# Reordering the first loads, adding filler matmuls and fixing two GpSimd steps in a fused retention and adapter kernel

## The chip, the core and the metric

The kernel runs on one core of a Trainium2 chip. The core has five engines with a queue each. TensorE (PE in the profile, with its weight loads as PEld) multiplies matrices. VectorE (DVE) and ScalarE (ACT) move and combine tiles. GpSimd (POOL) does slower elementwise work and issues its own DMAs. SyncE (SP) does nothing here but issue DMAs. The metric is the device time of one execution in microseconds (us); lower is better.

## The reference: what is computed

Two parts follow each other. The first is causal retention for 8 batches, 8 heads, 576 positions and head size 64, all fp32:

```python
scores = scale * np.matmul(q, k.transpose(0, 1, 3, 2))
Dmat = np.where(rel >= 0, gamma[:, None, None] ** rel[None, :, :], 0.0)   # rel = i - j
attn = np.matmul(scores * Dmat, v)
x = attn.transpose(0, 2, 1, 3).reshape(4608, 512)
```

The second is a mixture of eight low-rank adapters. Each row x gets gate logits `x @ w_gate`. The two largest are kept and weighted by a softmax over the two, and the row receives `x + sum of w_e * (x @ A[e]) @ B[e]`, where A[e] is 512 x 16 and B[e] is 16 x 512.

## The kernel before, in words

The 576 positions are cut into four chunks of 128 and one of 64. A chunk of four batches is a "quad", which is loaded together, and two batches of a quad are a "unit". `units` lists 16 full units and, for the last chunk, two of half length. Every unit goes through lettered stages. T transposes q and k on PE with the identity `id64`. S multiplies kT by qT into `ps`, and DVE applies the causal mask (`rt`). U accumulates the state `pu` from k and v. Q multiplies the carried state P by qT. R multiplies rt by v into `px`, and DVE scales that into `xT`. Z multiplies `xT` by the packed adapter matrices and gate weights `AW` (`pz`), V and W route, B and X transpose, and Y multiplies by `Bcat` (the B matrices as fp16) and stores the rows.

PE, DVE and ACT instructions are emitted through `mm`, `vec` and `act` (lines 80 to 87). Each of them calls `chain` (line 73), which ties an instruction to the one before it on the same engine, so the order on these three engines is that of the source. GpSimd instructions are emitted directly, with `gp.`, and are not chained: there the framework's scheduler picks the order within what the data allow. SP's DMAs go out in the order in which the program places them.

The steps that matter here all lie in the first 45 us:

- `issue(0)` (line 195) loads the first quad in pieces: q and k of batch 0, of batch 1, then v of both, then the adapter matrix A (`load_A`, line 170), then q, k and v of batches 2 and 3. Its local `load` takes the issuing engine as an argument; k of batches 0 and 1 goes through ACT's queue (line 230), all else through SP's. `issue(1)` and later calls load a whole quad, 1 MB for each of q, k, v, from SP.
- At line 651 `spin(10)` sends ten fp16 matmuls of a zero tile (`idle`) into an unused bank (`spare`), ahead of the first real work.
- `first_T` (line 295) transposes the first unit batch by batch: q of batch 0, k of batch 0, q of batch 1, k of batch 1, eight transposes each. ACT copies qT out of the accumulators and DVE copies kT.
- `scale_k` (line 253) makes GpSimd scale k in place, one instruction for a batch, after PE has transposed it. `stage_U` needs the scaled k.
- `fill_pick` (line 620) builds the selector `pick` on GpSimd in four steps. `place_A` (line 173) uses it on PE to lay A out, and ACT copies the result into `AW[0]`. The gate weights are loaded straight into `AW[0]` by a GpSimd DMA (line 655). GpSimd then copies `AW[0]` with its halves swapped into `AW[1]` (lines 669 and 670), and line 671 loads `Bcat` with a GpSimd DMA that converts to fp16.
- After the first four units, lines 699 to 703 make two small masks `maskh` on GpSimd, which nothing uses before the last two units.

Of the kernel before, what the change touches and what calls it, by code (L numbers as in the profile page):

```python
# [18 lines left out]
def kernel(  # L19
# [10 lines left out]
    nc = tc.nc  # L30
# [26 lines left out]
    for hp in range(HP):  # L57
        for ho in range(2):
            g = gam[2 * hp + ho]
            r = slice(64 * ho, 64 * ho + 64)  # L60
# [12 lines left out]
    def chain(eng, i):  # L73

        i = getattr(i, "ins", i)
        if eng in queued:
            tc.add_manual_dep(i, queued[eng].name, order, reason="program order")
        queued[eng] = i

    def mm(*args, **kw):  # L80
        chain("pe", nc.tensor.matmul(*args, **kw))  # L81
# [20 lines left out]
    def bank(shape, name, dtype=FP32):  # L102

        n = free.pop(0)
        x = pp.tile(shape, dtype, tag=f"bank{n}", name=name)
        held[id(x)] = n, x
        return x

    def done(*tiles):
        free.extend(held.pop(id(x))[0] for x in tiles)  # L110
# [5 lines left out]
    gp = nc.gpsimd  # L116
# [3 lines left out]
    for base in (0, -L):  # L120
        gp.affine_select(
            out=id64, in_=id64, compare_op=ALU.not_equal, fill=1.0, base=base,
# [4 lines left out]
        out=tri, in_=tri, compare_op=ALU.is_ge, fill=0.0, base=0,  # L127
# [6 lines left out]
        out=ident16, in_=ident16, compare_op=ALU.not_equal, fill=1.0, base=0,  # L134
        pattern=[[-1, 128]], channel_multiplier=1,
    )
    for g in range(2):
        gp.tensor_copy(
            out=trih[64 * g : 64 * g + 64], in_=tri[64 * g : 64 * g + 64, 64 * g : 64 * g + 64]
# [7 lines left out]
    def spin(n):  # L147

        for _ in range(n):
            mm(spare, lhsT=idle[:, 0:128], rhs=idle, start=True, stop=True)  # L150
# [11 lines left out]
    AW = [  # L162
        cpool.tile([128, HP, ER + E], FP32, tag=f"AW{g}", name=f"AW{g}") for g in range(2)
    ]
    Bcat = cpool.tile([128, Dm], FP16, tag="Bcat", name="Bcat")
# [4 lines left out]
    def load_A():  # L170
        nc.sync.dma_start(out=Arow, in_=moe_A.rearrange("e (p l) r -> p e (l r)", l=4))
# [23 lines left out]
    def issue(n):  # L195
        if n >= len(quads):
            return
        c, qd = quads[n]
        first = n == 0
        tl = [  # L200
            iop.tile([128, QUAD, H, Dh], FP32, tag=tag, name=tag, bufs=n)
            for tag, n in (("q32", 2), ("k32", 3), ("v32", 3))
        ]
        if c == NFULL:
            if qd > 0:
                return
            for src, dst in zip((q, k, v), tl):
                for g in range(2):
                    nc.sync.dma_start(
                        out=dst[64 * g : 64 * g + 64].rearrange("p s h d -> p (s h) d"),  # L210
                        in_=src[HALF * g : HALF * g + HALF, :, C * c : C * c + L, :].rearrange(
                            "s h j d -> j (s h) d"
                        ),
                    )
            for u in range(2):
                nat[(c, u, 0)] = [x[:, 2 * u : 2 * u + 2] for x in tl]
            return

        def load(n, lo, hi, eng=nc.sync):
            eng.dma_start(  # L220
                out=tl[n][:, lo:hi].rearrange("p b h d -> p (b h) d"),
                in_=(q, k, v)[n][
                    QUAD * qd + lo : QUAD * qd + hi, :, C * c : C * c + C, :
                ].rearrange("b h j d -> j (b h) d"),
            )

        if first:
            for b in range(2):
                load(0, b, b + 1)
                load(1, b, b + 1, nc.scalar)  # L230
            load(2, 0, 2)
            load_A()
            for n in range(3):
                load(n, 2, 4)
        else:
            for n in range(3):
                load(n, 0, 4)
        for sl in range(2):
            nat[(c, qd, sl)] = [x[:, 2 * sl : 2 * sl + 2] for x in tl]
# [7 lines left out]
    def rows(g):  # L247
        return slice(64 * g, 64 * g + 64)
# [46 lines left out]
    def first_T():  # L295

        s = st.setdefault(0, {})
        for nm in ("qT", "kT"):
            s[nm] = wk.tile([128, 2, HP, C], FP32, tag=nm, name=nm, bufs=4 if nm == "qT" else 2)
        for b in range(2):  # L300
            for n, nm in enumerate(("qT", "kT")):
                src = nat[units[0]][n]
                ps = [bank([128, HP, L], f"p{nm}") for _ in range(2)]
                for hp in range(HP):
                    for g in range(2):
                        mm(
                            ps[g][:, hp, :],
                            lhsT=src[rows(g), b, 2 * hp : 2 * hp + 2, :],
                            rhs=id64[rows(g), :],
                            is_transpose=True,  # L310
                            start=True,
                            stop=True,
                        )
                for g in range(2):
                    o = s[nm][:, b, :, rows(g)]
                    if n == 0:
                        act("copy", out=o, in_=ps[g])
                    else:
                        vec("tensor_copy", out=o, in_=ps[g])
                done(*ps)  # L320

    def stage_Q(t):
        c, qd, sl = units[t]
# [296 lines left out]
    def fill_pick(*dts):  # L620
# [9 lines left out]
        out=asc[0].rearrange("p a (m n) -> p a m n", n=NI),  # L630
# [16 lines left out]
    for t in range(NU):  # L647
        if units[t][2] == 0:
            issue(quads.index(units[t][:2]) + 2)
        if t == 0:  # L650
            spin(10)
            first_T()
            scale_k(0)
            fill_pick(3)
            gp.dma_start(
                out=AW[0][:, :, ER : ER + E], in_=moe_w_gate.rearrange("(t p) e -> p t e", p=128)
            )
            for ho in range(2):
                act("copy", out=asc[1][rows(ho)], in_=asc[0][rows(1 - ho)])
            act(  # L660
                "copy", out=gdec.rearrange("p a b d -> p a (b d)"),
                in_=gde.unsqueeze(2).broadcast_to((128, HP, 2 * Dh)),
            )
            stage_S(0)
            stage_U(0)
            stage_Q(0)
            stage_R(0)
            place_A()
            for ho in range(2):
                gp.tensor_copy(out=AW[1][rows(ho)], in_=AW[0][rows(1 - ho)])  # L670
            gp.dma_start(out=Bcat, in_=moe_B.rearrange("e r d -> (e r) d"))
            stage_T(1, ("qT",))
            stage_T(1, ("kT",), shared=True)
            scale_k(1)
            stage_Z(0)
            stage_S(1)
            stage_W(0)
            stage_U(1)
            stage_Q(1)
            stage_R(1)  # L680
            stage_T(2, ("qT",))
            stage_B(0)
            stage_X([0])
            stage_Z(1)
            stage_V(1)
            stage_Y(0, spread=True)
            stage_T(2, ("kT",), shared=True)
            stage_T(3)
            scale_k(2)
            scale_k(3)  # L690
            stage_S(2)
            stage_W(1)
            stage_S(3)
            for u in (2, 3):
                stage_U(u)
                stage_Q(u)
                stage_R(u)
            late_T(4)
            for ho in range(2):
                gp.tensor_tensor(  # L700
                    out=maskh[ho], in0=trih.unsqueeze(1).broadcast_to((128, HP, L)),
                    in1=heads(1, ho, L), op=ALU.mult,
                )
            continue
        if t < 4 or units[t][2] or not is_full(t):
            continue

        before, near = [u for u in (t - 4, t - 3) if u > 0], (t - 2, t - 1)
        here = (t, t + 1)
        for u in here:  # L710
            for b, nm in enumerate(("qT", "kT")):
                stage_S(u, (b,))
                if t > LATE:
                    stage_T(u + 2, (nm,))
            if t > LATE:
                scale_k(u + 2)
        for u in before:
            stage_B(u)
        stage_X(before)
        stage_Z(near[0])  # L720
        stage_V(near[0])
        for u in before:
            stage_Y(u)
        stage_Z(near[1])
        stage_V(near[1])
        if units[t][0] > 0:
            for u in here:
                stage_Q(u)
        for u in near:
            stage_W(u)  # L730
        for u in here:
            stage_U(u)
            if units[t][0] == 0:
                stage_Q(u)
            stage_R(u)
        if t <= LATE:
            late_T(t + 2)

    h, n = NU - 2, NU - 1
# [66 lines left out]
```

## Time and profile before

| What | us |
|---|---|
| Median of five runs (lowest 184.71, highest 187.22) | 185.24 |
| The profiled execution, whole | 187.22 |
| Its span, from the first to the last instruction | 185.5 |
| PE busy in the span | 175.3 |
| DVE busy | 115.5 |
| ACT busy | 66.7 |
| POOL busy | 58.1 |

In the profile, a row of the timeline gives the start, the length, the engine, the line, the operation, and the tiles as "written <- read"; "x8" means eight instructions merged, and the bracket tells how long the engine had been idle before and what ended the wait. Line 81 is `mm`, line 84 `vec` and line 87 `act`, so PE, DVE and ACT rows are told apart by tile names. Matmuls overlap, so a group's length includes the tail of its last one; the distance between the starts of two groups is what PE spends on the first. The profiled execution is the slowest of the five, 1.98 us above the median, and about 1.7 us of its time lie outside the span.

### The profile page before, as it was taken

The page shows a single profiled execution, that of the slowest core. Times are in us where ns is not written, and L with a number is a line of the kernel's source. Part 1 is how long each engine was busy: PE and PEld are TensorE (multiplying, and loading weights), DVE is VectorE, ACT ScalarE, POOL GpSimd, SP SyncE. Part 2 cuts the span into 40 slices and gives each one's busy share as a digit, 9 for nine tenths or more (in the row PEclk, how much of TensorE's full clock was granted, in tenths as well). Part 3 has the DMA queues.
Part 4 walks back from the last instruction along what each step waited for, and adds up shares of the span by engine and source line. Part 5 has one row for each costly group of instructions (what it writes and reads, how often), then busy time and mean ns, then how long its engine had stood idle before and what let it go on. Part 6 is the DMA issues. An engine that isn't in the chain of part 4 may idle for free. (4 is left out here: it accounts for less than half of the span.)

```text
span 185.5 us, 8103 instructions
## 1 busy us (share of the span) xinstructions
PE 175.3 (94%) x3606; PEld 163.8 (88%) x3606; DVE 115.5 (62%) x294; ACT 66.7 (36%) x179; POOL 58.1 (31%) x69
## 2 busy tenths in 40 slices
PE   7997999969999999999999999999999999999970
PEld 2796999959999999999999999999999999999850
DVE  3684956967578745866267816792578347485660
ACT  3512146024412334087511753075406460132440
POOL 8685108026016600588022621453050004000000
PEclk9999999999999999999999999999999999999995
DMA  6999898869698989797899899998940050033185
GB/s 145 278 248 248 238 299 236 223 168 291 183 302 237 286 258 282 201 287 259 245 283 348 256 255 323 253 202 178 255 151 4 0 222 11 4 111 124 58 256 144
DMA packets 53283, 38.74 MB, mean 209 GB/s; under 512 B 26992, under 2 KB 48640, under 8 KB 53248
## 3 DMA queue, kind: packets, MB, share of 16 engines
q1 hardware_dynamic: 50688, 37.23, 71.0%
q10 hardware_dynamic: 2384, 0.85, 1.8%
q8 instruction: 28, 0.46, 1.1%
q0 software_dynamic: 176, 0.15, 0.5%
q14 instruction: 7, 0.06, 0.1%
HBM read 28.91 MB, written 9.44 MB: 207 GB/s over the span
## 5 line engine op out<-in xcount | busy, mean ns | idle before, releaser
L84 DVE TENSOR_TENSOR rt<-ps,mask 128x512 f32<-128x512 f32 x64 | 40.3, 684 | 9.2 <-PE ps L81 8.0
L259 POOL TENSOR_TENSOR k<-k,pack 128x512 f32<-128x512 f32 x32 | 32.6, 1043 | 28.2 <-PE pkT L81 21.3
L81 PE MATMUL pz<-AW,xT 128*128 128x136 f32 x288 | 37.2, 282 | 0.0
L418 POOL TENSOR_TENSOR P<-pn,gdec 128x512 f32<-128x512 f32 x12 | 15.3, 1278 | 68.5 <-DVE pn L84 64.3
L81 PEld LDWEIGHTS pz<-AW,xT 128*128 128x128 f32 x288 | 34.7, 190 | 0.2
L81 PE MATMUL ps<-qT,kT 64*128 64x128 f32 x512 | 34.7, 278 | 0.1
L81 PEld LDWEIGHTS ps<-qT,kT 64*128 64x128 f32 x512 | 31.4, 188 | 1.2 <-issue 0.5
L81 PE MATMUL px<-rt,v 128*64 128x128 f32 x512 | 30.7, 273 | 0.0
L87 ACT COPY qT<-pqT 128x512 f32<-128x512 f32 (+1 forms) x33 | 16.8, 568 | 31.4 <-PE pqT L81 31.4
L81 PEld LDWEIGHTS px<-rt,v 128*64 128x64 f32 x512 | 27.7, 137 | 0.0
L84 DVE TENSOR_TENSOR xT<-px,asc 128x512 f32<-128x512 f32 x36 | 24.4, 689 | 3.9 <-PE px L81 2.6
L87 ACT COPY kT<-pkT 128x512 f32<-128x512 f32 x29 | 16.0, 600 | 29.4 <-PE pkT L81 18.7
L84 DVE COPY lg<-pz 128x16 f32<-128x16 f32 x17 | 3.0, 174 | 32.9 <-PE pz L81 32.9
L81 PE MATMUL pu<-v,k 128*64 128x64 f32 x512 | 18.1, 224 | 0.0
L87 ACT COPY osb<-po 128x256 f32<-128x256 f32 x60 | 17.5, 386 | 1.4 <-PE po L81 0.8
L81 PEld LDWEIGHTS pu<-v,k 128*64 128x64 f32 x512 | 16.6, 138 | 1.4 <-issue 1.0
L87 ACT ACTIVATE sg<-lg,ns 128x8 f32<-128x8 f32 x34 | 8.4, 293 | 25.3 <-DVE ns L84 24.9
L81 PE MATMUL pkT<-id,k 64*128 64x64 f32 x288 | 13.3, 227 | 3.1 <-DMA k<-in_k_dram 3.0
L81 PEld LDWEIGHTS pkT<-id,k 64*128 64x128 f32 x288 | 11.7, 141 | 4.3 <-issue 2.2
L81 PE MATMUL px<-qT,P 64*64 64x128 f32 (+1 forms) x512 | 14.2, 259 | 0.0
L84 DVE TENSOR_TENSOR pn<-pu,P 128x512 f32<-128x512 f32 x12 | 8.3, 692 | 8.3 <-PE pu L81 8.3
L81 PEld LDWEIGHTS px<-qT,P 64*64 64x64 f32 x512 | 12.5, 133 | 0.9
(54 smaller groups left out, 151.6 us busy)
## 6 DMA issues: line engine op xcount, KB each, us to landing
out_dram<-osb SPq DMA_DIRECT2D x32, 256.0 KB, 4.2
v<-in_v_dram SPq DMA_DIRECT2D x4, 512.0 KB, 7.1
q<-in_q_dram SPq DMA_DIRECT2D x3, 512.0 KB, 5.3
k<-in_k_dram SPq DMA_DIRECT2D x3, 512.0 KB, 8.4
out_dram<-osb SPq DMA_DIRECT2D x6, 128.0 KB, 2.3
q<-in_q_dram SPq DMA_DIRECT2D x2, 256.0 KB, 4.2
k<-in_k_dram ACTq DMA_DIRECT2D x2, 256.0 KB, 4.6
Arow<-in_moe_A_dram SPq DMA_DIRECT2D x1, 256.0 KB, 6.5
```

The lines of the kernel that those rows point to most:

```text
L81: chain("pe", nc.tensor.matmul(*args, **kw))
L84: chain("dve", getattr(nc.vector, fn)(**kw))
L87: chain("act", getattr(nc.scalar, fn)(**kw))
L259: gp.tensor_tensor(out=kk[:, b], in0=kk[:, b], in1=gv[:, 0].unsqueeze(2).broadcast_to((128, H, Dh)), op=ALU.mult,)
L418: nc.gpsimd.tensor_tensor(out=Pt, in0=pn, in1=gdec, op=ALU.mult)
```

## The change

Three edits are made.

- `load` loses its engine argument, and k of the first two batches is loaded from SP. SP's queue then holds q0, k0, q1, k1, v, A and the rest, in that order, and ACT's queue holds only the small constant `pack`.
- In `first_T`, two filler matmuls of the same kind as those of `spin(10)` follow each group of eight transposes but the last: six fillers in all, between q0 and k0, k0 and q1, q1 and k1.
- The two copies into `AW[1]` and the load of `Bcat` are chained to each other on GpSimd, so that the load comes after the copies.

```diff
-        def load(n, lo, hi, eng=nc.sync):
-            eng.dma_start(
+        def load(n, lo, hi):
+            nc.sync.dma_start(
...
             for b in range(2):
                 load(0, b, b + 1)
-                load(1, b, b + 1, nc.scalar)
+                load(1, b, b + 1)
...
                 done(*ps)
+                if (b, n) != (1, 1):
+                    spin(2)
...
             for ho in range(2):
-                gp.tensor_copy(out=AW[1][rows(ho)], in_=AW[0][rows(1 - ho)])
-            gp.dma_start(out=Bcat, in_=moe_B.rearrange("e r d -> (e r) d"))
+                chain("pool", gp.tensor_copy(out=AW[1][rows(ho)], in_=AW[0][rows(1 - ho)]))
+            chain("pool", gp.dma_start(out=Bcat, in_=moe_B.rearrange("e r d -> (e r) d")))
```

The scheduler answers with another order on GpSimd than the diff alone tells. The queue's order from the first step of `pick` to the second unit's scaling of k is:

```
before: pick, k0, pick, k1, pick, load gate weights, pick, load Bcat, maskh, maskh, AW[1] x2, k of unit 1
after:  pick, load gate weights, pick, k0, pick, maskh, pick, k1, maskh, AW[1] x2, load Bcat, k of unit 1
```

(k0 and k1 are the scalings of the first two batches.) On DVE the order does not change, on ACT only the two DMA issues leave, and on PE only the fillers come in.

## The prediction

> **What bounds the kernel now.** I read the page's slices first, because they tell which stages have room.
>
> ```profile
> PE 175.3 (94%) x3606; PEld 163.8 (88%) x3606; DVE 115.5 (62%) x294; ACT 66.7 (36%) x179; POOL 58.1 (31%) x69
> PE   7997999969999999999999999999999999999970
> DMA  6999898869698989797899899998940050033185
> ```
>
> A slice is 4.64 us. PE is full nearly everywhere; the room is in the first slice, in the fourth (13.9 to 18.6 us), in the ninth (37.1 to 41.7 us) and at the end. The change touches the first 20 us only, so the question is how a shift of PE made there travels through the fourth and ninth slices. The waits of PE say what those are.
>
> ```profile
> PE pkT L81 <- DMA k<-in_k_dram: 3.0, 2, 1.7
> ```
>
> Two waits for a load of k, 3.0 us together. The timeline gives their places and the whole head.
>
> ```profile
> 1.26 4.45 PE L81 MATMUL spare<-idle 128*128 128x512 f16 x10 [1.26 <-DVE warm L152]
> 5.64 0.69 PE L81 MATMUL pqT<-id,q 64*128 64x64 f32 x8
> 6.12 0.64 PE L81 MATMUL pkT<-id,k 64*128 64x64 f32 x8
> 6.55 0.64 PE L81 MATMUL pqT<-id,q 64*128 64x64 f32 x8
> 6.87 1.04 POOL L259 TENSOR_TENSOR k<-k,pack 128x512 f32<-128x512 f32 x1 [1.56 <-PE pkT L81]
> 7.13 0.47 PE L81 MATMUL pkT<-id,k 64*128 64x64 f32 x8
> 7.69 2.06 PE L81 MATMUL ps<-qT,kT 64*128 64x128 f32 x32
> 7.87 0.63 POOL L622 TENSOR_SCALAR_AFFINE_SELECT pick<-pick 128x512 f32<-128x512 f32 x1
> 8.47 1.04 POOL L259 TENSOR_TENSOR k<-k,pack 128x512 f32<-128x512 f32 x1
> 9.68 1.15 PE L81 MATMUL pu<-v,k 128*64 128x64 f32 x32
> 10.05 0.94 POOL L655 DMA_DIRECT2D AW<-in_moe_w_gate_dram  x1
> 10.66 1.92 PE L81 MATMUL px<-rt,v 128*64 128x128 f32 x32
> 11.57 0.57 POOL L671 DMA_DIRECT2D Bcat<-in_moe_B_dram  x1
> 12.16 1.20 POOL L700 TENSOR_TENSOR maskh<-trih,pack 128x256 f32<-128x256 f32 x2
> 15.63 0.71 PE L81 MATMUL pkT<-id,k 64*128 64x64 f32 x16 [1.31 <-DMA k<-in_k_dram]
> 15.83 1.31 POOL L670 COPY AW<-AW 64x544 f32<-64x544 f32 x2 [2.46 <-DMA AW<-in_moe_w_gate_dram]
> 16.28 2.12 PE L81 MATMUL pz<-AW,xT 128*128 128x136 f32 x16
> 39.94 0.71 PE L81 MATMUL pkT<-id,k 64*128 64x64 f32 x16 [1.68 <-DMA k<-in_k_dram]
> ```
>
> The reader is to see three things. PE runs from 1.26 to 14.3 us with almost no hole: the ten fillers end at 5.64, and when the transposes want q1 and k1, these have just landed (issue plus landing time puts q0, k0, q1, k1 at 4.0, 5.3, 6.4 and 7.1). PE then waits 1.31 us for the second k of the quad, and 1.68 us before 39.94 for the k of the third quad. After 39.9 PE is busy 134.91 of 135.10 us to 175. So a microsecond that PE loses before 14 us is paid for only as far as these waits don't hold it, and the end of the kernel hangs on when the k load of 39.8 lands.
>
> **Fillers.** Ten take 4.45 us, start to start 0.43. Six at that price are 2.6 us. But the clock doubles in this stretch: eight transposes take 0.43 from start to start at 6.12 and about 0.25 after 7.13 (a single one 311 ns before, 221 after). The Trainium skill (TensorE: Matmul & The Clock Gate, "What's actually happening") says that the gate opens after one busy window of about 3.4 us, and that the windows run free. From a start at 1.26 that allows an opening from 4.7 to 8.1; this trace has it near 7.0. The rule speaks against the fillers: PE is busy already, so they cannot open the gate sooner, they can only stand in the path. By the row (opening at 7.0): two fillers at 0.43 after q0, k0's transposes start at 6.97 instead of 6.12 and end at 7.4; four fillers at half the price (0.22; two 128x256 fp16 matmuls of Y, 0.11 apart at full clock, are one filler) and sixteen transposes at 0.03 follow, and S starts at 7.4 + 4 x 0.22 + 0.5 = 8.8 instead of 7.69: 1.1 late. By the rule's two ends: opening at 4.7 lets the fillers fall into waits for the loads (0 late); at 8.1 nearly 1.5 late. I take 1.1.
>
> **Loads.** The skill (DMA: Bandwidth & Descriptors, "Issuing engines are not separate DMA queues") says that a second issuing queue saves only the sequencer's time. This trace agrees in rate: 288 and 290 GB/s in the two microseconds from 5 to 7 with both queues and 288 from 7 to 8 with SP's alone. So the same bytes move. v no longer takes a share ahead of k1: pack, q0, k0, q1 and k1 are 1.11 MB, at 0.285 MB/us from 2.2 us with a slow start and 0.4 us to landing, so k1 comes at about 6.5 instead of 7.1. That is worth nothing, as PE with its fillers comes after that. SP pays two issues of 0.56 us more, but its next one, A, is held 3.57 us because the queue is full, which hides them; if that cover were gone, later loads would slip by 1.1 us.
>
> **GpSimd.** This is the part which costs. k1 now stands behind two more instructions than before: of pick's steps all four, and one maskh, come ahead of it. Before, it ended at 9.5, ahead of U at 9.68. After: pick ends at 5.31 as now, the gate load's issue takes 0.94 (6.25), pick 0.63 (6.9), k0 waits for the transposes of batch 0 (7.6) and takes 1.04 (8.65), then pick 0.60, maskh 0.60, pick 0.60, and k1 1.04: 11.5. U needs k1 from its third product on, so 28 of its 32 matmuls, 0.86 us, come after 11.5, and R starts at about 12.4 instead of 10.66. The fillers' 1.1 us lie inside this: S started at 8.8 ends at 10.8 and waits. They overlap and aren't added. R is 1.75 us late, bounds 1.3 (k0 scaled at once after 6.9) and 1.85 (GpSimd steps slowed by DVE, as pick's first one was, 1.09 against 0.63).
>
> **Where the 1.75 us go.** A's products start at 12.51 + 1.75 = 14.26, the second unit's q transposes at 15.36 and its k transposes at 15.9. The k load has landed by 15.5, so PE waits no more: 15.9 against 15.63, 0.3 late. Z needs the gate weights (now loaded about 4 us sooner) and AW[1]: A's four copies on ACT end about 0.8 after A's products, at 16.2; GpSimd copies until 17.5; Z's second half wants it at 15.9 + 0.65 + 1.03 = 17.6. Just met. Then Bcat's issue (0.57) stands ahead of the scaling of the second unit's k, 2.04: done at 20.2, wanted by U at 20.6. Met with 0.4 to spare. Y wants Bcat at 26.6, and with its 5.2 us to landing it is there at 23.3. So PE carries 0.3 to the wait that ends at 39.94, which holds 1.68. At that point nothing is left, if k lands when it did.
>
> **Bcat's place.** From 14 to 15 us, while it moved, the DMAs delivered 204 GB/s against 283 at 10 us; about 0.27 MB of the loads, 0.9 us, were put off. Later it puts off other loads by the same, for it still moves before 39.8. Its value lies between 0 and -0.9 (it falls into stretches in which the queues run low: the load rate falls to 77 GB/s from 20 to 21 us). I take 0, since SP is held by a full queue in each load from A on, so that the loads' chain is one of amounts, and the amounts are equal.
>
> **The sum.** Against the profiled execution of 187.22: +1.75 at R, -1.45 in the wait at 15.6, -0.3 in that at 39.9: 187.2. The median is 1.98 lower, and its waits for loads may be shorter than the profile's, so I add 0.3: 185.5.
>
> **Rivals.**
> 1. Absorbed, as above: 185.5, and 184.9 to 186.2. Chance 0.57.
> 2. Slower, since U's wait for k1 reaches the end. Place: GpSimd's queue ahead of U. Price 1.75, or 2.3 if the gate opens late and all fillers are slow. It decides where the two load waits together hold less than that; they hold 3.0 in the profiled execution, but that one is 2 us slower than the median, and that difference may be just these waits. 185.24 + 1.75 = 187.0, up to 187.6. Against it: in the fourth slice the gate weights (15.7) and AW[1] (17.1) hold Z about as long as k does. Chance 0.23.
> 3. The single queue is slower to fill: SP's two added issues push every later load by 1.1, and the k of 39.9 with them: 186.3; with the extra share of a lagging DMA engine 187.5. For it: at 37 to 39 us little moves (39 and 23 GB/s) though the load isn't complete. Chance 0.08.
> 4. Faster: Bcat's 0.9 us fall into gaps, and the k of 39.8 lands that much earlier: 184.3. At most 1.68 - 0.3 = 1.4, 183.8. Chance 0.12.
>
> **Range and chances.** 184.2 to 187.5 leaves out the tails of 2 and 3 and the end of 4. A measurement of this kernel tells about 1%, 1.85 us, from no change. Over 1% slower is half of case 2, part of 3 and a remainder, 0.22; over 1% faster hardly comes out of any step, 0.06; within 1% is 0.72.
>
> **What would show it.** In the changed profile: a wait of PE (or its weight loads) for POOL k inside U, near 10.8, of 0.5 to 1 us; R from about 12.4; no wait for k at 15.6; the gate load issued near 5.3 and Bcat's near 17.6; a wait for k before 39.9 that is shorter by 0.3, with the same end. The forecast is wrong if that k lands at another time than 39.8 by more than 1 us, if the second unit's U waits for its scaled k, or if PE is late at 38.2 by more than the wait.

## The result, and the profile after

The changed kernel takes 186.32 us (median; the kernel before, run beside it, 185.10). The ratio is 1.0073, with a 95% interval of 1.0057 to 1.0090: slower by about 1.3 us. That is inside the forecast range and within 1%, but it is not the absorbed change that the forecast put first. Executions that take 1.5% or more above the fastest of their kernel are left out of the ratios but not of the medians, and the one of 187.22 us whose profile stands before the prediction is such an execution. Of the profile's page for the changed kernel, the lines that answer to those of before are these.

```profile
PE 176.7 (96%) x3612; PEld 163.6 (88%) x3612; DVE 115.6 (62%) x294; ACT 66.7 (36%) x179; POOL 58.6 (32%) x69
PE   7999999999999999979999999999999999999970
DMA  6998979998599999698799899999920050033175
```

The low slices at 14 and 37 us are gone, so PE is fuller, and yet the time is longer. A new low slice, near 81 us, is a hole of 0.99 us that is taken up below. The timeline of the same execution shows the head.

```profile
1.26 4.40 PE L81 MATMUL spare<-idle 128*128 128x512 f16 x10 [1.26 <-DVE warm L152]
5.60 0.46 PE L81 MATMUL pqT<-id,q 64*128 64x64 f32 x8
5.99 0.60 PE L81 MATMUL spare<-idle 128*128 128x512 f16 x2
6.53 0.46 PE L81 MATMUL pkT<-id,k 64*128 64x64 f32 x8
...
8.76 2.27 PE L81 MATMUL ps<-qT,kT 64*128 64x128 f32 x32
...
10.12 1.03 POOL L259 TENSOR_TENSOR k<-k,pack 128x512 f32<-128x512 f32 x1
...
12.07 1.92 PE L81 MATMUL px<-rt,v 128*64 128x128 f32 x32
...
15.58 0.67 PE L81 MATMUL pkT<-id,k 64*128 64x64 f32 x16
...
16.17 2.39 PE L81 MATMUL pz<-AW,xT 128*128 128x136 f32 x16
```

S starts at 8.76 and R at 12.07, with no wait at the second unit's k transposes. Against the profile of before that the forecast used, this looks nearly harmless: 15.58 stands against 15.63. But before_a and before_b, two further profiles of the kernel before, of executions of 184.07 and 184.16 us, give another comparison. They lie about 1 us under its median. The first one's timeline:

```profile
7.47 2.26 PE L81 MATMUL ps<-qT,kT 64*128 64x128 f32 x32
9.66 1.15 PE L81 MATMUL pu<-v,k 128*64 128x64 f32 x32
10.64 1.92 PE L81 MATMUL px<-rt,v 128*64 128x128 f32 x32
...
14.50 0.72 PE L81 MATMUL pkT<-id,k 64*128 64x64 f32 x16 [0.18 <-DMA k<-in_k_dram]
15.14 2.13 PE L81 MATMUL pz<-AW,xT 128*128 128x136 f32 x16
17.20 2.06 PE L81 MATMUL ps<-qT,kT 64*128 64x128 f32 x32
...
37.08 0.71 PE L81 MATMUL pkT<-id,k 64*128 64x64 f32 x16
```

Here the wait at the second k is 0.18 us, not 1.31, and the wait at 39.9 doesn't exist: the third quad's k transposes start at 37.08. The view of PE's waits says the same in one line; the 0.8 us are the waits at 7.17 (0.62) and 14.50 (0.18).

```profile
PE pkT L81 <- DMA k<-in_k_dram: 0.8, 2, 0.6
```

### The profile page after: what moved, and what is told of

Read it like the earlier page. It is cut to its first block, busy times and chain, and to the rows that moved or that the text cites. A ratio compares the mean times of both kernels' runs of the same rounds, so it can differ in the third digit from the quotient of the medians.

```text
span 184.9 us, 8115 instructions
## 1 busy us (share of the span) xinstructions
PE 176.7 (96%) x3612; PEld 163.6 (88%) x3612; DVE 115.6 (62%) x294; ACT 66.7 (36%) x179; POOL 58.6 (32%) x69
## 5 line engine op out<-in xcount | busy, mean ns | idle before, releaser
L81 PEld LDWEIGHTS ps<-qT,kT 64*128 64x128 f32 x512 | 30.8, 188 | 2.4 <-issue 1.9
L81 PE MATMUL pkT<-id,k 64*128 64x64 f32 x288 | 12.8, 225 | 0.1
L81 PEld LDWEIGHTS pkT<-id,k 64*128 64x128 f32 x288 | 11.2, 139 | 1.9 <-issue 1.4
```

## The experiments

All ran beside the kernel before. "Ratio" is to the kernel before, with its 95% interval; it is not the quotient of the medians, and the text goes by it.

| Run | Edit | Median, us | Ratio |
|---|---|---|---|
| after_again | changed kernel, again | 186.75 | 1.0080 (1.0049 to 1.0111) |
| after_c | changed kernel, a third time | 186.30 | 1.0070 (1.0045 to 1.0096) |
| fill_only | the fillers alone | 186.26 | 1.0051 (1.0023 to 1.0079) |
| queue_only | the queue edit alone | 185.61 | 1.0032 (1.0007 to 1.0058) |
| pool_only | the GpSimd chain alone | 185.29 | 1.0016 (0.9987 to 1.0045) |
| no_fill | changed kernel without fillers | 186.24 | 1.0039 (1.0010 to 1.0068) |
| k_first | changed kernel, k scaled first | 186.21 | 1.0076 (1.0049 to 1.0102) |
| spin4 | changed kernel, four fillers each | 187.60 | 1.0131 (1.0080 to 1.0182) |
| gate_act | before, gate load on ACT's queue | 185.69 | 1.0035 (1.0010 to 1.0061) |
| before_a | before itself | 185.17 | 1.0013 (0.9977 to 1.0049) |
| before_b | before itself | 185.33 | 1.0004 (0.9978 to 1.0031) |
| deep | before, one more load buffer | 212.17 | 1.1448 (1.1389 to 1.1507) |

**The change's parts.** Four runs came first: the changed kernel again, and each edit alone.

> The changed kernel itself, a second time, for a second profile. Theory S (the head): what the change costs is made before 40 us: R starts about 1.4 us later, 0.33 us of that is left at the second unit's S, and loads of k no longer stop PE; then 1.2 to 1.4 us over before must be seen as PE being later at 38 us in a kernel before whose own load waits are small. Theory G (the gap): the first profile has a hole of 0.99 us in PE inside an S group at 81.65 us, with no releaser, which before has not; 0.33 from the head and 1.0 from the hole make the 1.3 us. G expects the hole again at the same place, within 0.2 us of its size; S expects no hole or one elsewhere, and the same time all the same.

The hole near 81 us did not come again, so theory G, that fillers lengthen the instruction stream and so cause it, falls for this kernel. Holes of this kind came without fillers too (0.54 us at 75.0 in gate_act, 0.40 us at 75.5 in no_fill); what makes them wasn't found. R starts at 11.87. This execution also shows U waiting for the scaled k, as step "GpSimd" of the forecast had it (the timeline's rows of U):

```profile
10.16 0.34 PE L81 MATMUL pu<-v,k 128*64 128x64 f32 x4
11.00 1.03 PE L81 MATMUL pu<-v,k 128*64 128x64 f32 x28 [0.50 <-POOL k L259]
```

Four of U's 32 products run, and 28 wait for k1.

```diff
+                if (b, n) != (1, 1):
+                    spin(2)
```

> Only the six fillers; loads and GpSimd chain as before. The scheduler again puts k1's scaling behind other GpSimd steps (the gate load ahead, Bcat's load in place of one maskh). S and G both expect nearly the whole cost here, +1.0 to +1.5 us over before: R 1.3 to 1.8 late, 0.3 or more left after Z, and (G) the hole of 1 us near 81 us, since PE's stream is longer by the same 24 instructions. If the queue edit were the cause: 0.

The fillers alone, with the GpSimd order that comes with them, cost 0.51%, 0.9 us, somewhat under the span expected; the interval, 0.4 to 1.5 us, holds most of that span. S started at 9.30 and R at 12.48 in the profiled execution, which took 187.28 us, 1.0 over its median, and waited 1.23 us for the third quad's k. GpSimd's order moved with the fillers alone: k1 was scaled from 9.87 on.

```diff
-                load(1, b, b + 1, nc.scalar)
+                load(1, b, b + 1)
```

> Only the loads of k0 and k1 moved to SP's queue. S and G: 0 within 0.4 us, k1 lands no later than 7.1 us by more than 0.5, GpSimd's order as before. The rival that the single queue is slower to fill: +1.0 us, with the k of the second unit and of the third quad landing 1 us later.

R started at 10.72, so the head was nearly as before, and the time still rose by 0.32%, with an interval that lies wholly above 1. That is a miss for S and G, though less than the rival's 1.0 us. The view of busy time by stage, for 4 to 7 us, gives in its last column the rate of the loads in GB/s. First queue_only:

```profile
4.00:7.00 3.00, 2.34 (x29) 1.16 (x26) 2.00 (x3) 1.14 (x4) 2.74 (x4) 1.00 1.14 259
```

and before_a, with two queues:

```profile
4.00:7.00 3.00, 2.55 (x29) 1.18 (x26) 2.65 (x4) 0.98 (x5) 2.02 (x3) 1.00 1.27 286
```

In the same window six profiles with k0 and k1 on ACT's queue (three of before, pool_only, fill_only, gate_act) show 281 to 287 GB/s, and all seven with one queue 229 to 260. The deep run below has two queues as well and shows 218, so the queues alone don't set this rate. From 2 to 4 us the single queue was ahead, 249 to 256 GB/s against 228 to 241 in those six; over 2 to 7 us it is 237 to 257 against 261 to 268. k1 landed at 7.21 against 7.13 and 7.02, and the second k of the quad at 14.67 against 14.36 and 14.49 (queue_only against before_a and before_b). In this execution PE also waited for a k late in the kernel:

```profile
81.41 0.71 PE L81 MATMUL pkT<-id,k 64*128 64x64 f32 x16 [1.46 <-DMA k<-in_k_dram]
```

But before_a and before_b had no such wait, while the third profile of after, below, had none there either. So that wait looks like a thing of the execution.

```diff
-                gp.tensor_copy(out=AW[1][rows(ho)], in_=AW[0][rows(1 - ho)])
-            gp.dma_start(out=Bcat, in_=moe_B.rearrange("e r d -> (e r) d"))
+                chain("pool", gp.tensor_copy(out=AW[1][rows(ho)], in_=AW[0][rows(1 - ho)]))
+            chain("pool", gp.dma_start(out=Bcat, in_=moe_B.rearrange("e r d -> (e r) d")))
```

> Only the chain of the AW[1] copies and Bcat's load. S and G: 0 within 0.4 us. The rival that Bcat's later place helps the loads: -0.5 to -0.9 us, the second k of the first quad landing at about 14.7 instead of 15.5 us.

No difference can be told. The second k landed at 15.03 in its profile, not at 14.7, so Bcat's later place bought nothing that shows. This profile is of 184.87 us, nearer to a median of the kernel before than before_a and before_b. PE waited 0.70 us for the second k, and its eighth xT is at 38.02 us (37.27 and 37.39 there).

**Fillers, the k scaling, the gate load.** The second four runs.

```diff
                 done(*ps)
-                if (b, n) != (1, 1):
-                    spin(2)
```

> The changed kernel without its six fillers: loads in one queue and the GpSimd chain stay. GpSimd's order is then that of before up to the gate load: k1 is scaled ahead of it. Theory S (the fillers carry the cost, themselves and by moving k1's scaling back): R starts at 10.7 to 10.8 us as before, and the time is that of before within 0.5 us (184.7 to 185.6), about 1 us under the changed kernel. Rival Q (the single queue is slow): still +1.0 us or more over before.

R is back at 10.72, as S said. But the time is 0.39% over before, 0.7 us: outside S's span and under Q's 1.0 us, though the interval (0.2 to 1.3 us) reaches into both. So something is lost without the fillers, as in queue_only, and the two intervals agree. The same intervals don't tell no_fill from fill_only: how the cost is shared between fillers and queue isn't shown.

k_first chains the later steps of `pick` and the gate load, the latter ahead of the third step of `pick`, then k0 and k1, then the fourth step and both maskh (the lines at their old places go):

```diff
-            gp.tensor_tensor(
+            i = gp.tensor_tensor(
...
+            if t == 0:
+                chain("pool", i)
...
+    chain("pool", gp.dma_start(
+        out=AW[0][:, :, ER : ER + E], in_=moe_w_gate.rearrange("(t p) e -> p t e", p=128)
+    ))
     fill_pick(2)
...
+            for ho in range(2):
+                chain("pool", gp.tensor_tensor(
+                    out=maskh[ho], in0=trih.unsqueeze(1).broadcast_to((128, HP, L)),
+                    in1=heads(1, ho, L), op=ALU.mult,
+                ))
             place_A()
```

> The changed kernel with GpSimd's order fixed so that both scalings of the first unit's k follow each other as soon as the gate load and three steps of pick are issued, and the maskh steps come after them. Theory S splits the 1.1 to 1.4 us by which R is late in the changed kernel: the fillers themselves put S 0.3 to 1.1 late, the wait of U for k1 adds 0.1 to 0.7. So here U runs on from S without a hole, R is 0.3 to 1.1 late, and the time lies 0.1 to 0.5 us under the changed kernel. If the wait for k1 were the whole cause: that of before, 185.2.

No gain can be told: 1.0076 against the changed kernel's 1.0073, with intervals that would hide the 0.1 to 0.5 us expected. U ran on from S without a hole, as expected, but S itself started at 9.30, because the matmuls were still slow: the first two fillers between transposes took 0.40 us each (6.26 to 7.07), against 0.27 in the first profile of after. The lower end of the interval, 0.9 us over before, leaves no room for the wait for k1 as the whole cause, and hardly as the main one.

```diff
-                    spin(2)
+                    spin(4)
```

> The changed kernel with four fillers instead of two after each group, six more in all. Each costs 0.22 (clock gate open) to 0.43 us: S comes 1.3 to 2.6 us later than in the changed kernel. What of the first 1.4 us was covered at Z is used up, so theory S expects the time to rise by the same 1.0 to 2.0 us over the changed kernel: 187.4 to 188.5. If fillers were hidden by waits for loads: no rise, 186.4.

187.60, by the medians 1.3 us over the changed kernel, inside what S expected, near its lower end; by the ratios 1.1 us, give or take about 1. Six more fillers at 0.22 us, the price with the gate open, are 1.3 us. So these fillers seem to be paid for in full, hidden neither by waits for loads nor by anything at Z.

```diff
     issue(0)
+    nc.scalar.dma_start(
+        out=AW[0][:, :, ER : ER + E], in_=moe_w_gate.rearrange("(t p) e -> p t e", p=128)
+    )
     issue(1)
...
-            gp.dma_start(
-                out=AW[0][:, :, ER : ER + E], in_=moe_w_gate.rearrange("(t p) e -> p t e", p=128)
-            )
```

> The kernel before with one edit: the gate weights are loaded from ACT's queue behind k1, at about 2.5 us, and not from GpSimd at 10. It asks whether the gate load holds Z up in the kernel before (it landed at 15.2 to 15.7 us, Z started at 15.8 to 16.3). If it does: Z starts as soon as the second unit's k is transposed and AW[1] is copied from 14.6 on, 0 to 0.4 us earlier, time -0.2 to -0.5 us (184.7 to 185.0). If the load of k alone holds Z: 0.

It missed: 0.35% slower. The gate weights landed at 9.32 instead of 14.6, AW[1] was copied from 14.52 on, and Z started at 15.57, not before the 15.14 and 15.27 of before_a and before_b. The second k landed at 14.80 and held Z. Why it is slower and not the same stays open. As this edit costs as much as the queue edit, some of queue_only's 0.32% may come with any small change of the program; no run tells the two apart.

**The kernel before again, the changed one again, deeper loads.** The last four.

before_a and before_b have no edit.

> The kernel before itself, for a profile of an ordinary execution, and as a control of the comparison: the ratio should be 1.000 with about 0.3% to either side. Theory P (PE's head plus a few waits for loads): the time is made of where PE stands at the eighth xT (38.0 to 38.4 us here), of waits for loads between 38 and 94 us, and of a tail that is the same in all kernels (78.8 us from the 17th to the last xT). At 185.1 us the load waits after 38 us come to under 1.0 us together, and there is no wait of 1.7 us at 39.9.

> The same once more, for a second profile: R from 10.6 to 10.8 us, the tail 78.8 us again, load waits after 38 us under 1.0 us if its time is near 185.1. If the waits differ from the first profile's by more than 0.3 us, they are a thing of the execution and not of the kernel.

Both as expected by P, and the control's ratio is 1 within its interval. But both profiled executions are 1 us faster than the median and have no load wait after 15 us, so what an execution at the median waits for there wasn't seen.

> The changed kernel a third time. Theory P: R 1.1 to 1.8 us later than in the two profiles of before, 0.4 to 0.9 us left at the eighth xT, the tail 78.8 us, and the rest of the 1.3 us in waits for loads between 38 and 94 us. Rival H (all in the head): the eighth xT at least 1.2 us later than in before, and no difference after it.

The eighth xT lies 1.85 us later than in before, which is H's first number and beyond P's; H's second, no difference after it, does not hold for this execution, as 1.6 us more are lost there. Part of it is a wait for the third quad's k, just behind the eighth xT, and part a hole of 0.52 us at 64.1:

```profile
39.66 0.71 PE L81 MATMUL pkT<-id,k 64*128 64x64 f32 x16 [0.60 <-DMA k<-in_k_dram]
```

The table sets before_a and before_b beside the three of the changed kernel (start, us):

| Mark | before_a, before_b | after, after_again, after_c | Mean difference |
|---|---|---|---|
| S, first unit | 7.47, 7.36 | 8.76, 7.97, 9.35 | 1.28 |
| R, first unit | 10.64, 10.53 | 12.07, 11.87, 12.52 | 1.57 |
| k transposes, second unit | 14.50, 14.62 | 15.58, 15.36, 16.03 | 1.10 |
| S, second unit | 17.20, 17.32 | 18.50, 18.29, 18.95 | 1.32 |
| eighth xT | 37.27, 37.39 | 38.72, 38.51, 39.18 | 1.47 |
| last xT | 171.86, 171.88 | 174.40, 173.48, 175.34 | 2.54 |

At the eighth xT the changed kernel is 1.47 us late, and the timed difference is 1.2 to 1.5 us. After that the changed kernel's three executions lose 0.4 to 1.6 us more. But two of them lie over the median (186.58 and 187.57), and both of before lie 1 us under theirs, so the last row's 2.54 overstates the difference. The best match is after_again, whose 185.65 us is 0.7 under the changed kernel's median: 1.18 us late at the eighth xT and 1.61 at the last. So the head holds most of the difference there; in an execution at the median, how much of it lies in the head isn't shown. From the 17th xT to the last, PE's work takes 78.8 us in all five.

The deep run took `bufs` of q, k and v from 2, 3, 3 to 3, 4, 4, issued one quad further ahead, and shortened the unused tile `warm` to make room.

```diff
-            for tag, n in (("q32", 2), ("k32", 3), ("v32", 3))
+            for tag, n in (("q32", 3), ("k32", 4), ("v32", 4))
...
-            issue(quads.index(units[t][:2]) + 2)
+            n = quads.index(units[t][:2])
+            issue(n + 2) if n == 0 else None
+            issue(n + 3)
```

> The kernel before with one more buffer for q, k and v, loading three quads ahead instead of two from the fourth quad on. It takes away what makes k of the later quads late (their loads stand behind stores and wait for q's buffer). Theory P: no wait of PE for a load between 45 and 90 us, and where before loses time there, it gains it: 0 to -0.8 us against before. If there are no such waits in before: 0. Slower if loads that now stand ahead of the first stores hold those up until the output buffers run out.

It is 14% slower, and so it can't tell anything about load waits in the kernel before. PE waited 7.1 us for loads of k instead of 0.8. Its longest wait, 10.8 us, for which the profile shows no cause ("issue"), ended at 114.26 us, shortly after what the expectation's last sentence named: ACT's wait, up to 113.52, for a store to leave the output buffer.

```profile
PE pu L81 <- issue: 11.1, 2, 10.8
ACT osb L87 <- DMA out_dram<-osb: 14.3, 2, 12.4
```

## Why the prediction was half right

That the number fell inside 184.2 to 187.5 is due to the width of the range. The favoured account was missed: 186.3 lies over its 184.9 to 186.2, and one of the forecast's own signs of being wrong came, a k of the third quad that lands more than 1 us away from 39.8 (37.84 and 37.30 in after and after_again).

**The clock gate and the fillers** held in the main. The gate opened at different times in different executions, so S was 0.5 to 1.9 us late by the three profiles; 1.1 was the taken value and 1.28 the mean. The two ends, 0 and 1.5, were too low. The earliest opening, which the forecast worked out from the Trainium skill (TensorE: Matmul & The Clock Gate, "What's actually happening") as one window of 3.4 us after the start, was too late: in after_again the spacing of the first ten fillers fell from 427 to 217 ns at about 4 us, 2.7 us after PE's start. The profile's granted clock is 1.00 all through these microseconds and doesn't show it; the weight loads of the fillers do (up to 3.80 each row is one of them, and then three take 0.58 us):

```profile
3.37 0.15 PEld L81 LDWEIGHTS <-idle 128*128 128x128 f16 x1 [0.28 <-issue]
3.80 0.58 PEld L81 LDWEIGHTS <-idle 128*128 128x128 f16 x3 [0.28 <-issue]
```

**GpSimd and U** held in place, not in size. k1's scaling ended at 11.15 in the first profile of after, against 11.5. R was 12.07, 11.87 and 12.52, against about 12.4. "They overlap and aren't added" is seen in the three executions: U waited 0.50 us for k1 where S was early (7.97), and not at all where S was late (9.35). From S to R the three took 3.31, 3.90 and 3.17 us, against 3.17 in before_a and before_b: on average the order of k1 added 0.3 us to the fillers' 1.28. So it was the fillers that made most of R's delay, and not GpSimd, which the forecast called "the part which costs". What no run shows is what the k1 order would cost alone, without fillers.

**"Where the 1.75 us go" failed**, and with it "the sum", which let 1.45 us vanish in the wait at 15.6 and the rest in that at 39.9. The size of R's delay was 1.57 instead of 1.75. Measured against before_a and before_b, its cover at the second k was 0.35 and 0.59 us instead of 1.45 (from q's transposes to k's they take 0.90 and 1.14 us, the changed kernel 0.55), and at the third quad there was none, since k lands at 14.4 to 14.5 there, not 15.5, and the third quad's k at 36.1 and 36.5, not 39.8. In pool_only, nearer to the median, the cover at the second k would be 0.86. The forecast had the sign of this in hand, as it called the profiled execution 1.98 us slower than the median and put "these waits" down as a possible reason. It still took the covers at full size for the likeliest case and allowed 0.3 us. Rival 2 has the right path, R's delay that reaches the end, but not the right place, U's wait for k1; its 187.0 was 0.7 too high. About 0.5 us of R's delay did go before the second unit's k transposes, where PE had waited a little; Z and R of the second unit added some again, 0.27 and 0.16 (below).

**"Just met" for Z** was a little short. In the changed kernel Z's second half waits for AW[1] on PE's weight loads, and Z lasts 2.33 us (16.17 to 18.50) against 2.06 (15.14 to 17.20).

```profile
17.37 0.99 PEld L81 LDWEIGHTS pz<-AW,xT 128*128 128x128 f32 x8 [0.21 <-POOL AW L672]
```

**The second unit's k scaling** met U, but it collided elsewhere: it now runs from 17.94 to 19.98, over the routing steps on DVE. The timeline's rows of GpSimd and DVE, first of after, then of before_a:

```profile
17.94 2.04 POOL L259 TENSOR_TENSOR k<-k,pack 128x512 f32<-128x512 f32 x2
19.08 0.92 DVE L84 SCALAR_TENSOR_TENSOR ns<-m 128x2 f32<-128x2 f32 x1
```

```profile
16.11 2.05 POOL L259 TENSOR_TENSOR k<-k,pack 128x512 f32<-128x512 f32 x2
17.79 0.37 DVE L84 SCALAR_TENSOR_TENSOR ns<-m 128x2 f32<-128x2 f32 x1
```

In both the step ended when GpSimd's multiplication did, at 20.00 and at 18.16. In queue_only, where GpSimd was done as the step began (18.09), it took 0.16 us. The masks of S behind it started later, and R of the second unit took 2.01 us from start to start instead of 1.85, in all three profiles of the changed kernel. The forecast counted GpSimd's steps but not what they hold up on DVE.

**"Loads"** failed in its rate. It took the single queue to move as much as two from a later stretch (288 GB/s from 7 to 8 us). Between 4 and 7 us one queue moved 229 to 260 GB/s, two 281 to 287. k1 came at 7.05 to 7.33, not at 6.5, and the change that was costed at nothing costs 0.32% in queue_only (0.07 to 0.58). The issues were mis-sized as well: SP spent 0.9 to 1.2 us on that of q1 and 0.85 to 1.1 on that of k1, not 0.56, and v was issued at 3.8 to 4.1 us instead of 1.93. The Trainium skill says in the section weighed there (DMA: Bandwidth & Descriptors, "Issuing engines are not separate DMA queues") that a second issuing engine saves only the time of issuing. The rates alone don't contradict it, as these later issues may be what lowers them; no run separates the two. So part of rival 3 may be right, at about half its price: 0.6 us. The path to these 0.6 us isn't shown: the second k is only 0.2 to 0.6 us later in queue_only and no_fill.

**Bcat's place** held: 0, and the pool_only interval leaves -0.2 to +0.8 us.

Added up, the fillers' 0.51% and the queue's 0.32% make 0.83%, beside 0.73% measured, well within the intervals. That the fillers cost something is shown by fill_only; the queue's share rests on an interval that lies only just above no change.

## What to carry to other kernels

Before a wait is used as a cover, look at whether the profiled execution is an ordinary one: where it lies 1% above the median, its waits for loads are the first suspects, and the delay should be costed with and without them. Filler work that an engine does in its own program order is paid for as soon as the data are there: here six fillers more cost about what they take. A scheduler that picks the order on an unchained engine may answer an edit on another engine, so read the order of every queue, and then what each moved step shares its time with.

## What the runs showed that was not expected

In six profiles two queues fed the first small loads 8 to 25% faster than one from 4 to 7 us (281 to 287 against 229 to 260 GB/s); over 2 to 7 us it was 2 to 13%. The clock gate opened as early as 2.7 us after PE's first matmul and as late as about 5.8 us (in after_c the pair of fillers at 6.26 still took 0.86 us up to 7.12, where that of after, at 5.99, took 0.54), in executions of kernels with the same start. A DVE step on a tile of 128 x 2 took 0.92 us instead of 0.16 and ended with the GpSimd multiplication beside it. In the deep run the loads moved only 230 GB/s from 2 to 7 us, where before_a moved 267, though the queues held the same loads up to then; by the edit only the tiles' places in memory and their number differed. The cause was not looked for.
